# Half of one row tile of w2 sent to partitions 0 to 63 by two 32-partition transfers

## The chip, the cores and the metric

The kernel runs on one core of one Trainium2 chip. The metric is the device time of one execution in microseconds (us); the time before is 774.0 us, the median of three runs (773.93 to 774.09). All data is float32.

## What is computed

One decoding step (batch 2, one token each, model width D = 1024). The input x is normalised, and three terms are added: x itself, an attention term over a cache of 32768 positions (4 key/value heads, 32 query heads of width 128), and a feed-forward term with hidden width F = 3584:

```python
xn = _layernorm(x)
h  = silu(xn @ w1)              # w1 is 1024 x 3584
out = x + attention(xn, k_cache, v_cache, wq) @ wo + h @ w2   # wo 4096 x 1024, w2 3584 x 1024
```

The caches and the weights are 331 MB, each read once; every token's arithmetic is small beside that.

## The kernel before, in words

Everything large passes through three buffers of 128 partitions x 64 KB (bufA, bufB, bufC), filled by transfers that SyncE issues in program order (function `load`, line 205; each transfer has a semaphore of its own count). First wq and w1 are streamed and multiplied: `first(u)` makes a [32 x 512] product per column block, `second(u)` turns it with identity matmuls so that the hidden values stand on partitions; line 194 copies them to `pre`, and lines 213 to 219 make hT = silu of them, one column group of 32 per row tile of 128 hidden values (28 tiles). Then eight loop turns stream the keys and values. After the loop the 32 row tiles of wo and the 28 row tiles of w2 (each 128 rows x 1024 columns, 4 KB per partition) are multiplied by oT and hT.

The work around the change is this tail. SyncE issues the pieces in the order of lines 344 to 346 and 376; the queue is one, so pieces move in that order. bufA is filled last: w2's tiles 16 to 27 in pieces of 1024 KB (four, two tiles each), 512 KB (tiles 24, 25 and 26, one each), and the last tile, 27, in four pieces of 128 KB. Each piece has a semaphore, and TensorE waits for it just before the tile that needs it (line 359). Tiles up to number 55 of the 60 (wo's 32 count first) add into a [128 x 512] sum `acc2`, in two halves of 512 columns; VectorE adds the residual to it once (line 368, result in `ob`). Tiles 56 to 59 add into `acc`, [128 x 256]: four groups of 32 output partitions, group j holding columns 256 j to 256 j + 255 of the result. Just before tile 58 the matmuls of lines 356 to 358 fold `ob` into `acc` and so wait for VectorE. Tile 57, w2's third last (row tile 25), is multiplied at lines 370 and 371: four matmuls of 256 columns, all 128 partitions. The last tile is multiplied in four steps of 64 columns per group, one for each 128 KB piece (lines 382 to 386). Then ScalarE copies `acc` to `ot` (line 388) and stores it (line 389).

One float32 matmul of the code stands as two MATMUL records in the trace, each with a weight load (PEld).

Of the kernel before, what the change touches and what calls it, by code (L numbers as in the profile page):

```python
# [8 lines left out]
B, HQ, HKV, SK, DH, D, F = 2, 32, 4, 32768, 128, 1024, 3584  # L9
P = 128  # L10
REP = HQ // HKV
W = 16384
# [2 lines left out]
SUB = 4096  # L15
N1 = F // 512
FT = F // P
QW = D // 4
LOOPS = HKV * B
EPS = 1e-5  # L20
# [31 lines left out]
        self.eng.sem_inc(token, -n)  # L52


def gqa_plus_mlp_kernel(nc, x, kt, v, wq, wo, w1, w2, out):


    pe, dve, act, pool = (Stream(nc, e, n) for e, n in
                          ((nc.tensor, "pe"), (nc.vector, "dve"), (nc.scalar, "act"), (nc.gpsimd, "pool")))
# [3 lines left out]
    def sem(name):  # L63
        sems.append(nc.alloc_semaphore(name))
        return sems[-1]

    def sb(name, *shape):
        return nc.alloc_sbuf_tensor(name, shape, F32).ap()

    def bank(name):  # L70
        return nc.alloc_psum_tensor(name, (P, 512), F32).ap()

    bufA, bufB, bufC = (sb(n, P, W) for n in ("bufA", "bufB", "bufC"))
    ldA, ldB, ldC, ldx, ldr, done = (sem(n) for n in ("ldA", "ldB", "ldC", "ldx", "ldr", "done"))
    tq, tps, trm, tgd, te, tls, tob = (sem(n) for n in ("tq", "tps", "trm", "tgd", "te", "tls", "tob"))
    ident, ones, sel, fold = sb("ident", P, P), sb("ones", P, P), sb("sel", P, 32), sb("fold", P, 64)
# [4 lines left out]
    stats, mv, ln = sb("stats", B, 2, nc.vector.BN_STATS_DIM), sb("mv", B, 2), sb("ln", B, 6)  # L81
    qall = sb("qall", P, LOOPS, REP)
    qT = sb("qT", P, 160)
    oT, hT = sb("oT", P, HQ, 32), sb("hT", P, FT, 32)
    pre, sig, rsig = (sb(n, P, FT, B) for n in ("pre", "sig", "rsig"))
    pr = [sb(f"pr{i}", P, 512) for i in range(2)]
    ob, ot = sb("ob", P, 512), sb("ot", P, QW)
    mx, ls = sb("mx", P, NC, REP), sb("ls", P, NC, REP)
# [4 lines left out]
    ps = [pair[a // 2][:, a % 2 * 512:(a % 2 + 1) * 512] for a in range(2 * NC)]  # L93
    po, acc, smA, smB = (bank(n) for n in ("po", "acc", "smA", "smB"))
    acc = acc[:, :QW]

    def mm(o, lhsT, rhs, start=True, stop=True):
        return nc.tensor.matmul(o, lhsT, rhs, start=start, stop=stop)  # L98
# [20 lines left out]
    V = nc.vector  # L119
# [5 lines left out]
    for i in range(2):  # L125
        t = dve.mark(V.bn_stats(stats[:, i, :], xt[:, i * 512:(i + 1) * 512]))
    dve.wait(t)
    t = dve.mark(V.bn_aggr(mv, stats))
    var, std, y0, t0, t1, rstd = (ln[:, i:i + 1] for i in range(6))
    dve.wait(t)  # L130
    t = dve.mark(V.tensor_scalar_add(var, mv[:, 1:2], EPS))
    act.wait(t)
    t = act.mark(nc.scalar.activation(std, var, AF.Sqrt))
    for f in (lambda: V.reciprocal(y0, std), lambda: V.tensor_mul(t0, y0, y0), lambda: V.tensor_mul(t1, t0, var),
# [4 lines left out]
        t = dve.mark(f())  # L139
# [5 lines left out]
    for k in range(KT):  # L145
        m = mm(px[:, k, :], xn[:, k * P:(k + 1) * P], ident[:B, :B])
    t = pe.mark(m)
# [27 lines left out]
    def second(u):  # L175

        parts = blocks[u][2]
        n = 32 * parts
        o = ps[2 + u % 2][:, :8 * parts].rearrange("p (i j b) -> p i j b", i=4, b=B)
        pe.wait(copied[u])  # L180
        if u >= 2:
            pe.wait(read[u - 2])
        for i in range(4):
            m = mm(o[:, i], pr[u % 2][:n, i * P:(i + 1) * P],
                   ident[:n, :n].rearrange("p (j m) -> p j m", m=32)[:, :, :B])
        dve.wait(pe.mark(m))
        if u < 2:
            for j in range(2):
                h = 2 * u + j
                m = V.tensor_copy(qall[:, B * h:B * (h + 1), :].rearrange("p b (j i) -> p b j i", j=2),  # L190
                                  o[:, :, 2 * j:2 * j + 2, :].rearrange("p i j b -> p b j i"))
        else:
            at = 16 * (u - 2)
            m = V.tensor_copy(pre[:, at:at + 4 * parts, :].rearrange("p (j i) b -> p j i b", i=4),
                              o.rearrange("p i j b -> p j i b"))
        read.append(dve.mark(m))

    for u in range(4):
        first(u)
        if u:  # L200
            second(u - 1)
    second(3)


    def load(buf, src, s, *ticks):
        for of, n in ticks:
            sp.wait_ge(of.sem, n)
        sp.dma_start(buf, src).then_inc(s, 16)  # L208
# [5 lines left out]
    t = act.mark(nc.scalar.activation(sig, pre, AF.Exp, scale=-1.0))  # L214
    for f in (lambda: V.tensor_scalar_add(sig, sig, 1.0), lambda: V.reciprocal(rsig, sig),
              lambda: V.tensor_mul(hT[:, :, ::16], pre, rsig)):
        dve.wait(t, zs)
        t = dve.mark(f())
# [28 lines left out]
    for it in range(LOOPS):  # L247
        h, b = divmod(it, B)
        for c in range(NC):
            dve.wait(tick(it, c))  # L250
            t = dve.mark(V.transpose(st[:, 2 * c:2 * c + 2].rearrange("p a j m -> p (a j m)"), pair[c]))  # L251
            dve.wait(t)
            m = V.tensor_reduce(mx[:, c, :], st[:, 2 * c:2 * c + 2].rearrange("p a j (r m) -> p m (a j r)", r=4),  # L253
                                AX.X, ALU.max)
            if c == 0:
                m.then_inc(tps, 1)
        m = dve.mark(m)
# [5 lines left out]
        t = dve.mark(V.tensor_reduce(gm, smA[:REP, :P], AX.X, ALU.max))  # L263
# [3 lines left out]
        t = dve.mark(V.tensor_copy(gmax[:, 0, :], smB[:, :REP]))  # L267
# [6 lines left out]
        for c in range(NC):  # L274
            dve.wait(tick(it, 4 + c))
            m = V.tensor_reduce(ls[:, c, :], e8[c].rearrange("p n m -> p m n"), AX.X, ALU.add)  # L276
# [6 lines left out]
        t = dve.mark(V.reciprocal(rl, smA[:, :REP]))  # L283
# [8 lines left out]
    with nc.tensor.While(lambda: nc.tensor.snap(turn) < LOOPS):  # L292
        pe.take(tq)
        for a in range(4):
# [4 lines left out]
            for r in range(4):  # L299
                for q4 in range(4):  # L300
                    n = (4 * (a % 2) + q4) * 4 + r
                    m = mm(ps[a][32 * q4:32 * q4 + 32, :], qT[:, 32 * r:32 * r + 32], buf[:, n * 512:(n + 1) * 512],
                           r == 0, r == 3)
# [6 lines left out]
        for a in range(4):  # L310
# [4 lines left out]
            for j in range(16):  # L315
                q4, n = j % 4, 16 * (a % 2) + j
                m = mm(po[32 * q4:32 * q4 + 32, :], st[:, a, j, :], buf[:, n * 512:(n + 1) * 512],
                       a == 0 and j < 4, a == 3 and j >= 12)
# [5 lines left out]
        for r in range(4):  # L324
            m = mm(smB[:, :REP], ob[:, r * P:(r + 1) * P], sel[:, REP * r:REP * (r + 1)], r == 0, r == 3)
# [8 lines left out]
    def stream(buf, src, cuts, *ticks):  # L334

        for lo, hi in zip(cuts, cuts[1:]):
            s = sem(f"piece{len(pieces)}")
            load(buf[:, lo:hi], src[:, lo:hi], s, *ticks)
            pieces.append((hi, s))
            yield hi, s  # L340

    lo = 11 * D
# [8 lines left out]
    def tiles(buf, ends, at, n):  # L351
        for i in range(n):
            t = at + i
            if t == PAIRED + 2:
                pe.wait(i_fold, i_sums)
                for j in range(4):
                    mm(acc[32 * j:32 * j + 32, :], fold[:, 32 * (j // 2):32 * (j // 2) + 32],
                       ob[:, (j % 2) * QW:(j % 2 + 1) * QW], False, False)
            pe.wait((next(s for hi, s in ends if hi >= (i + 1) * D), 16))
            lhsT, w = oT[:, t, :] if t < HQ else hT[:, t - HQ, :], buf[:, i * D:(i + 1) * D]  # L360
            if t < PAIRED:
                for half in range(2):
                    g = 2 * (t % 2) + half
                    m = mm(acc2[32 * g:32 * g + 32, :], lhsT, w[:, half * 512:(half + 1) * 512],
                           t < 2, t >= PAIRED - 2)
                if t == PAIRED - 1:
                    dve.wait(pe.mark(m), (ldr, 32))
                    i_sums = dve.mark(V.tensor_add(ob, acc2, xres))
            else:
                for j in range(4):  # L370
                    m = mm(acc[32 * j:32 * j + 32, :], lhsT, w[:, j * QW:(j + 1) * QW], t == PAIRED, False)
        return m

    pe.wait(i_oT, i_hT)
    i_wo0 = pe.mark(tiles(*plan[0], 16))
    ends = [*stream(bufA, w2[:, W:], (0, 2 * D, 4 * D, 6 * D, 8 * D, 9 * D, 10 * D, lo, lo + QW, lo + 2 * QW,
                                      lo + 3 * QW, lo + D), i_wo0)]
    for buf, loaded, at in plan[1:]:
        tiles(buf, loaded, at, 16)
    tiles(bufA, ends, 48, 11)  # L380
    f = QW // 4
    for u in range(4):
        pe.wait((ends[7 + u][1], 16))
        for j in range(4):
            m = mm(acc[32 * j:32 * j + 32, u * f:(u + 1) * f], hT[:, FT - 1, :],
                   bufA[:, lo + (4 * u + j) * f:lo + (4 * u + j + 1) * f], False, u == 3)
# [36 lines left out]
```

## Time and profile before

| | |
|---|---|
| median of 3 runs | 774.0 us |
| the profiled execution | 773.97 us |
| its span, first to last instruction | 772.5 us |
| outside the span | 1.47 us |
| HBM read | 331.37 MB, 429 GB/s over the span |
| TensorE busy | 52% |
| queue of SyncE, share of 16 DMA engines | 99.4% |

The page gives busy time by engine, the busy share of the 16 DMA engines in 40 slices, and the chain of work that ended last. Views with a window give the same for a stretch: the DMA share there is the mean over the 16 DMA engines of the time in which they move packets (it can stand a little over 1 in a short window, since a packet is counted whole in one place), and GB/s is what they moved. A timeline merges like instructions, gives the start of the first, how long the group took, and in brackets how long the engine stood idle before and what released it.

### The profile page before, as it was taken

To read this page: it belongs to the slowest core of one execution; us is meant where nothing else is said; L and a number is where in the kernel's file an instruction comes from. 1 tells how busy PE (TensorE), PEld (TensorE's weight loads), DVE (VectorE), ACT (ScalarE), POOL (GpSimd) and SP (SyncE) were. 2 spreads that over 40 slices of the span, in tenths; PEclk is the share of its full clock that TensorE was granted. 3 is DMA by queue.
4 is the path that set the end of the run, shared out by engine and by line. 5 is a ranking of instruction groups with operands and counts; after the bars stand their busy time and mean duration, and the time that the engine had idled before them with its cause. 6 is when DMAs were issued, how large, how long until landed. Compare 5 with 4: busy or idle time off the path is not lost. (4 is left out here: it accounts for less than half of the span.)

```text
span 772.5 us, 5904 instructions
## 1 busy us (share of the span) xinstructions
PE 404.3 (52%) x2736; PEld 127.9 (17%) x2736; DVE 120.7 (16%) x153; ACT 27.3 (4%) x33; POOL 3.0 (0%) x10
## 2 busy tenths in 40 slices
PE   1455545465446455545465446455545465446476
PEld 1111211121112111111121112111111121112111
DVE  2000013111311131113111311131113111311000
ACT  0000100000100010000000100000000000100000
POOL 1000000000000000000000000000000000000000
PEclk9966766766766766766766766766766766766768
DMA  9999999999999999999999999999999999999997
GB/s 388 434 432 432 434 435 434 435 434 434 434 434 434 435 434 431 434 434 434 431 431 434 434 434 434 434 434 434 434 434 431 434 434 434 434 434 434 418 418 320
DMA packets 7379, 331.48 MB, mean 429 GB/s; under 512 B 830, under 2 KB 1350, under 8 KB 1740
## 3 DMA queue, kind: packets, MB, share of 16 engines
q1 hardware_dynamic: 7344, 331.35, 99.4%
q8 instruction: 6, 0.10, 0.0%
q10 hardware_dynamic: 28, 0.02, 0.0%
q14 instruction: 1, 0.01, 0.0%
HBM read 331.37 MB, written 0.01 MB: 429 GB/s over the span
## 5 line engine op out<-in xcount | busy, mean ns | idle before, releaser
L98 PE MATMUL po<-bufB,st 128*32 128x512 f32 x512 | 75.5, 755 | 80.5 <-PEq L52 80.5
L98 PE MATMUL ps<-bufB,qT 128*32 128x512 f32 x512 | 75.0, 751 | 79.3 <-PEq L52 79.3
L98 PE MATMUL ps<-bufA,qT 128*32 128x512 f32 x512 | 75.6, 756 | 48.4 <-PEq L52 48.4
L98 PE MATMUL po<-bufA,st 128*32 128x512 f32 x512 | 74.4, 746 | 36.6 <-PEq L52 36.6
L276 DVE TENSOR_REDUCE ls<-st 128x8 f32<-128x1024 f32 x16 | 31.7, 1984 | 230.8 <-PE po L98 230.8
L251 DVE STREAM_TRANSPOSE st<-ps 128x1024 f32<-128x1024 f32 x16 | 20.0, 1250 | 248.0 <-PE ps L98 248.0
L98 PEld LDWEIGHTS po<-bufB,st 128*32 128x32 f32 x512 | 20.6, 135 | 135.3 <-issue 135.3
L98 PEld LDWEIGHTS ps<-bufB,qT 128*32 128x32 f32 x512 | 20.4, 134 | 133.8 <-issue 133.8
L98 PEld LDWEIGHTS ps<-bufA,qT 128*32 128x32 f32 x512 | 20.7, 135 | 96.7 <-issue 96.7
L98 PEld LDWEIGHTS po<-bufA,st 128*32 128x32 f32 x512 | 20.5, 134 | 83.9 <-issue 83.9
L253 DVE TENSOR_REDUCE mx<-st 128x8 f32<-128x1024 f32 x16 | 31.7, 1980 | 0.6
L273 ACT ACTIVATE st<-st 128x1024 f32<-128x1024 f32 x16 | 16.9, 1056 | 359.1 <-DVE st L272 358.5
L98 PE MATMUL ps<-bufB,xnT 128*32 128x512 f32 x112 | 18.5, 745 | 14.6 <-PEq L52 14.6
L98 PE MATMUL smA<-ident,rm 128*8 128x128 f32 x16 | 4.1, 348 | 29.4 <-PEq L52 29.4
L272 DVE TENSOR_TENSOR st<-st,gmax 128x1024 f32<-128x1024 f32 x16 | 18.9, 1221 | 0.3
L98 PE MATMUL ps<-bufC,oT 128*32 128x512 f32 x64 | 9.4, 753 | 10.5 <-DMA bufC<-in_wo 10.5
L98 PE MATMUL ps<-bufC,xnT 128*32 128x512 f32 x64 | 9.5, 758 | 10.1 <-DMA bufC<-in_w 10.1
L98 PE MATMUL smA<-lsum,ones 128*128 128x8 f32 x16 | 3.5, 291 | 19.2 <-PEq L52 19.2
L281 ACT COPY ob<-po 128x512 f32<-128x512 f32 x8 | 4.7, 585 | 237.9 <-PE po L98 237.9
L98 PE MATMUL smB<-sel,ob 128*128 128x8 f32 x64 | 13.0, 333 | 0.0
L98 PEld LDWEIGHTS smB<-sel,ob 128*128 128x128 f32 x64 | 12.6, 293 | 0.0
L98 PE MATMUL ps<-bufB,hT 128*32 128x512 f32 x64 | 9.6, 763 | 3.9 <-DMA bufB<-in_w 3.9
(65 smaller groups left out, 100.5 us busy)
## 6 DMA issues: line engine op xcount, KB each, us to landing
bufB<-in_w SPq DMA_DIRECT2D x1, 6144.0 KB, 25.5
bufB<-in_w SPq DMA_DIRECT2D x1, 5632.0 KB, 41.8
bufA<-in_w SPq DMA_DIRECT2D x4, 1024.0 KB, 35.4
bufB<-in_w SPq DMA_DIRECT2D x1, 2560.0 KB, 47.7
bufA<-in_w SPq DMA_DIRECT2D x3, 512.0 KB, 40.0
bufA<-in_w SPq DMA_DIRECT2D x4, 128.0 KB, 23.5
bufA<-in_kt SPq DMA_DIRECT2D x8, 29.2
bufB<-in_kt SPq DMA_DIRECT2D x8, 29.0
```

What stands on the lines that cost most here:

```text
L98: return nc.tensor.matmul(o, lhsT, rhs, start=start, stop=stop)
L251: t = dve.mark(V.transpose(st[:, 2 * c:2 * c + 2].rearrange("p a j m -> p (a j m)"), pair[c]))
L253: m = V.tensor_reduce(mx[:, c, :], st[:, 2 * c:2 * c + 2].rearrange("p a j (r m) -> p m (a j r)", r=4), AX.X, ALU.max)
L272: act.wait(dve.mark(V.tensor_sub(e8[c], e8[c], gmax.to_broadcast([P, 128, REP]))))
L273: nc.scalar.activation(e8[c], e8[c], AF.Exp, scale=SCALE).then_inc(te, 1)
L276: m = V.tensor_reduce(ls[:, c, :], e8[c].rearrange("p n m -> p m n"), AX.X, ALU.add)
L281: nc.scalar.copy(ob, po).then_inc(tob, 1)
```

## The change

The columns 512 to 1023 of w2's row tile 25 (256 KB: 128 rows of 2 KB) are no longer loaded as 128 partitions x 2 KB. They come from a new input w2x, in which row p and row p + 64 stand side by side: 64 rows of 4 KB, to bufA's columns 12 D to 13 D, partitions 0 to 63. Two transfers of 32 partitions each fetch them, and the source of each is written as eight groups of four rows that do not lie next to each other in memory (`"r e n -> e r n"`). The first half of the tile is loaded as before with rows of 2 KB in place of 4 KB. The tile's second half is then multiplied with 64 partitions at a time: two matmuls for each of the two column groups, in place of one. The hidden values of rows 64 to 127 of that tile are needed on partitions 0 to 63 too: `second(3)` gets one more matmul, and `pre`, `sig`, `rsig` and `hT` one more tile.

```diff
+LOW = FT - 3
-    oT, hT = sb("oT", P, HQ, 32), sb("hT", P, FT, 32)
-    pre, sig, rsig = (sb(n, P, FT, B) for n in ("pre", "sig", "rsig"))
+    oT, hT = sb("oT", P, HQ, 32), sb("hT", P, FT + 1, 32)
+    pre, sig, rsig = (sb(n, P, FT + 1, B) for n in ("pre", "sig", "rsig"))
...
+        if u == 3:
+            j, i = divmod(LOW - 16, 4)
+            xo = ps[2 + u % 2][:, 8 * parts:8 * parts + B]
+            m = mm(xo, pr[u % 2][:n, i * P + 64:i * P + 192], ident[:n, 32 * j:32 * j + B])
...
+            if u == 3:
+                m = V.tensor_copy(pre[:, FT, :], xo)
...
+            if t == HQ + LOW:
+                pe.wait(*((s, 16) for s in low))
...
                 for j in range(4):
+                    if t == HQ + LOW and j >= 2:
+                        for n in range(2):
+                            at2 = lowA + n * 512 + (j - 2) * QW
+                            m = mm(acc[32 * j:32 * j + 32, :], hT[:64, FT if n else LOW, :], bufA[:64, at2:at2 + QW],
+                                   False, False)
+                        continue
...
-    ends = [*stream(bufA, w2[:, W:], (0, 2 * D, 4 * D, 6 * D, 8 * D, 9 * D, 10 * D, lo, lo + QW, lo + 2 * QW,
-                                      lo + 3 * QW, lo + D), i_wo0)]
+    lowA, low = 12 * D, [sem("low0"), sem("low1")]
+    ends = [*stream(bufA, w2[:, W:], (0, 2 * D, 4 * D, 6 * D, 8 * D, 9 * D, 9 * D + D // 2), i_wo0)]
+    for n in range(2):
+        load(bufA[32 * n:32 * n + 32, lowA:lowA + D], w2x[n].rearrange("r e n -> e r n"), low[n])
+    ends += [(10 * D, ends.pop()[1])]
+    ends += [*stream(bufA, w2[:, W:], (10 * D, lo, lo + QW, lo + 2 * QW, lo + 3 * QW, lo + D))]
...
+    arrays["w2x"] = lay(arrays["w2"][:, LOW * D + D // 2:(LOW + 1) * D], (2, 2, 8, 4, D // 2), (1, 3, 2, 0, 4),
+                        (2, 4, 8, D))
```

## Rows read from the trace of the kernel before

**Rows 1.** The page: span, DMA in 40 slices, packets, queues.
```profile
span 772.5 us, 5904 instructions
...
DMA  9999999999999999999999999999999999999997
GB/s 388 434 432 432 434 435 434 435 434 434 434 434 434 435 434 431 434 434 434 431 431 434 434 434 434 434 434 434 434 434 431 434 434 434 434 434 434 418 418 320
...
q1 hardware_dynamic: 7344, 331.35, 99.4%
q8 instruction: 6, 0.10, 0.0%
```
**Rows 2.** Chain of waits from 766 us on: start us, us, what.
```profile
727.58 40.84 DMA bufA<-in_w
768.42 0.04 issue
768.46 0.99 PE acc L98 x24
...
769.48 0.68 PE acc L98 x16
```
**Rows 3.** Busy time by stretch, the last DMA work: columns in the first line.
```profile
core 0: us, PE busy (x) PEld busy (x) DVE busy (x) ACT busy (x) POOL busy (x), PEclk, DMA share, GB/s
...
767.00:767.50 0.50, 0.50 (x12) 0.22 (x12) 0.32 (x1) 0.00 (x0) 0.00 (x0) 0.69 1.03 356
767.50:767.75 0.25, 0.25 (x12) 0.15 (x8) 0.00 (x0) 0.00 (x0) 0.00 (x0) 1.00 0.80 283
767.75:768.00 0.25, 0.25 (x12) 0.06 (x4) 0.00 (x0) 0.00 (x0) 0.00 (x0) 1.00 0.53 180
768.00:768.25 0.25, 0.25 (x8) 0.00 (x0) 0.00 (x0) 0.00 (x0) 0.00 (x0) 1.00 0.50 172
768.25:768.50 0.25, 0.07 (x8) 0.04 (x6) 0.00 (x0) 0.00 (x0) 0.00 (x0) 1.00 0.46 160
768.50:768.75 0.25, 0.25 (x8) 0.12 (x8) 0.00 (x0) 0.00 (x0) 0.00 (x0) 1.00 0.40 139
768.75:769.00 0.25, 0.25 (x16) 0.18 (x8) 0.00 (x0) 0.00 (x0) 0.00 (x0) 1.00 0.36 123
769.00:769.25 0.25, 0.25 (x20) 0.17 (x12) 0.00 (x0) 0.00 (x0) 0.00 (x0) 1.00 0.27 94
769.25:769.50 0.25, 0.23 (x12) 0.07 (x10) 0.00 (x0) 0.00 (x0) 0.00 (x0) 1.00 0.02 4
```
**Rows 4.** The same view, while the 1024 KB and the 512 KB pieces move.
```profile
757.00:758.00 1.00, 1.00 (x16) 0.26 (x12) 0.00 (x0) 0.00 (x0) 0.00 (x0) 1.00 1.04 434
...
765.00:766.00 1.00, 1.00 (x8) 0.10 (x4) 0.00 (x0) 0.00 (x0) 0.00 (x0) 0.50 1.01 405
```
**Rows 5.** Timeline of weight loads from 764 us on.
```profile
764.62 0.20 PEld L98 LDWEIGHTS ps<-bufA,hT 128*32 128x32 f32 x8 [2.33 <-DMA bufA<-in_w]
765.90 0.15 PEld L98 LDWEIGHTS acc<-bufA,hT 128*32 128x32 f32 x4 [1.08 <-DMA bufA<-in_w]
...
767.18 0.19 PEld L98 LDWEIGHTS acc<-bufA,hT 128*32 128x32 f32 x8 [0.65 <-DMA bufA<-in_w]
767.47 0.34 PEld L98 LDWEIGHTS acc<-ob,fold 128*32 128x32 f32 x8
768.46 0.16 PEld L98 LDWEIGHTS acc<-bufA,hT 128*32 128x32 f32 x8 [0.66 <-DMA bufA<-in_w]
768.82 0.47 PEld L98 LDWEIGHTS acc<-bufA,hT 128*32 128x32 f32 x16 [0.20 <-DMA bufA<-in_w]
769.47 0.16 PEld L98 LDWEIGHTS acc<-bufA,hT 128*32 128x32 f32 x8 [0.18 <-DMA bufA<-in_w]
769.79 0.16 PEld L98 LDWEIGHTS acc<-bufA,hT 128*32 128x32 f32 x8 [0.16 <-DMA bufA<-in_w]
```
**Rows 6.** Timeline of TensorE's matmuls from 764 us on.
```profile
764.62 1.93 PE L98 MATMUL ps<-bufA,hT 128*32 128x512 f32 x8 [1.43 <-DMA bufA<-in_w]
766.33 1.53 PE L98 MATMUL acc<-bufA,hT 128*32 128x256 f32 x16
767.68 0.60 PE L98 MATMUL acc<-ob,fold 128*32 128x256 f32 x8
768.46 1.65 PE L98 MATMUL acc<-bufA,hT 128*32 128x256 f32 x40 [0.17 <-DMA bufA<-in_w]
```
**Rows 7.** Groups by shape from 745 us on: busy, mean ns of one | idle before.
```profile
L98 PE MATMUL acc<-ob,fold 128*32 128x256 f32 x8 | 0.6, 379 | 0.0
```
**Rows 8.** Timelines of VectorE and of ScalarE in the tail.
```profile
766.62 0.69 DVE L368 TENSOR_TENSOR ob<-ps,xres 128x512 f32<-128x512 f32 x1 [55.22 <-PE ps L98]
...
770.18 0.37 ACT L388 COPY ot<-acc 128x256 f32<-128x256 f32 x1 [62.88 <-PE acc L98]
770.58 0.64 ACTq L389 DMA_DIRECT2D out_y<-ot  x1
```
**Rows 9.** SyncE's issues of bufA's last pieces: timeline; page, us to landing.
```profile
724.84 33.22 SPq L208 DMA_DIRECT2D bufA<-in_w  x11
...
bufA<-in_w SPq DMA_DIRECT2D x4, 128.0 KB, 23.5
```
**Rows 10.** Timelines of TensorE and VectorE around `second(3)`.
```profile
86.24 1.95 PE L98 MATMUL ps<-ident,pr 128*128 128x8 f32 x16
96.85 9.46 PE L98 MATMUL ps<-bufA,qT 128*32 128x512 f32 x64 [8.66 <-PEq L52]
...
88.23 0.18 DVE L194 COPY pre<-ps 128x24 f32<-128x24 f32 x1 [0.70 <-PE ps L98]
```

More of the change, by code (lines that the diff above doesn't have):

```diff
@@ L52, in take, with gqa_plus_mlp_kernel @@
         self.eng.sem_inc(token, -n)
-def gqa_plus_mlp_kernel(nc, x, kt, v, wq, wo, w1, w2, out):
+def gqa_plus_mlp_kernel(nc, x, kt, v, wq, wo, w1, w2, w2x, out):
     pe, dve, act, pool = (Stream(nc, e, n) for e, n in
```

## Prediction, made before the changed kernel was run

> **What bounds the kernel now.** I read the page first: SyncE's queue fills 99.4% of what 16 DMA engines can do, every slice of the DMA line but the last stands at 9, and the rate is 434 GB/s nearly throughout [rows 1]. The change adds no bytes and takes none away, so it can't touch those 770 us; it can only touch how the stream ends. The chain of waits says the same: from 727.58 to 768.42 us it is one stretch of bufA's pieces, then TensorE's last matmuls [rows 2]. So next I cut the last microseconds into quarters. The reader is to see the DMA share there: 1.03 up to 767.5, 0.80, 0.53, then 0.50 at 768.00 to 768.25, and from there a slow fall to 0.02 after 769.25 [rows 3]. A share of 0.50 of 16 engines is eight engines at work and eight that have nothing left. SyncE's queue gave all sixteen the same bytes, so eight run behind the other eight by about 1.3 us, and the last pieces wait for those eight. The share summed from 767.75 on is 0.25 x (0.53 + 0.50 + 0.46 + 0.40 + 0.36 + 0.27 + 0.02) = 0.64 us. Spread evenly over sixteen engines the same work would end at 768.39 in place of about 769.26. So 0.87 us (0.11%) is the most that any redistribution of these bytes can bring, and the stake of the whole change.
>
> After the last packet TensorE follows closely: its last wait for a piece ends at 769.79 [rows 5], ScalarE's copy starts at 770.18 and the store is issued at 770.58 [rows 8]. That end, 0.39 us and what follows, stays as it is.
>
> **The change part by part.** The *transfers*. By the diff a half tile of 256 KB is taken from all 128 partitions and given to partitions 0 to 63 in rows of 4 KB, eight groups to a transfer. I read the eight groups as eight engines, each with four rows of each transfer; the trace of before has no such transfer, so bounds follow. Rates of one engine: rows of 8 KB, 434 GB/s at share 1.04, so 434 / (16 x 1.04) = 26.1 GB/s; rows of 4 KB, 405 / (16 x 1.01) = 25.1 [rows 4]; rows of 1 KB, 139 / (16 x 0.40) = 21.7 [rows 3]. For rows of 2 KB I take 24.4, between the last two and nearer the 4 KB row. Before, each engine moves 32 KB of the tile: 1.31 us. After, eight move 16 KB in rows of 2 KB, 0.67 us, and the other eight that and 32 KB in rows of 4 KB: 0.67 + 1.31 = 1.98 us. So eight engines gain 0.64 us and eight lose 0.67. If the eight that gain are those that are late, both groups end near 768.6 to 768.7 and the last landing is 0.6 us earlier. If any of those that lose is late, the end is 0.67 us later. From both sides: 0.87 us earlier (the sum above) to, with all of it on one engine, 256 KB / 25.1 = 10.4 us later; I take 0.6 us earlier, and say at the rivals why.
>
> Which partitions an engine serves no row here shows. The Trainium skill, "DMA: Bandwidth & Descriptors", sections "Why a DMA increments its semaphore by 16 and not by 1" and "The descriptor swizzle", gives the number of engines as the largest up to 16 that divides the slowest dimension of both sides, here 8, takes the lowest numbered ones, and has those write partitions 0 to 63. By it the reading above holds, and the engines that are relieved are numbers 8 to 15.
>
> *SyncE's queue*: two issues more, 13 in place of 11. The 11 take 33.22 us from 724.84, the last issue ending at 758.06, since the queue pushes back; the last pieces are issued a median 23.5 us ahead of their landing [rows 9]. Ten descriptors more on half of the engines, each of some 0.16 us (4 KB at 25.1), delay the last issue by 1 or 2 us, with over 9 us of cover. Nothing. Gone would be that cover only if the issue of the new form took some 9 us.
>
> *TensorE in the tail*. Tile 57 gets two matmuls more; column groups run side by side, so what counts is the longest group: four passes in place of two. A pass of 256 columns at a granted clock of 1.00 (2.4 GHz): the fold's 8 records take 0.60 us, one alone 0.379 [rows 6, 7], so its second pass starts 0.22 later. Two more passes: 0.44 us. Does that show? Tile 57 could start earlier, but TensorE works without a gap from 766.33 to 768.28 (766.33 + 1.53, then the fold, 767.68 + 0.60 [rows 6]), because up to 767 it runs at 0.50, 1.2 GHz [rows 3, 4]. So the fold moves from 767.68 to 768.12, past VectorE's sum, which is done at 766.62 + 0.69 = 767.31 [rows 8]. Tile 58 follows two passes later, at 768.56 (768.46 before, where it stood 0.17 us waiting for data [rows 6]); its data would be there at 767.9. It takes 0.44, so the first step of the last tile starts at 769.00, and each step has 8 weight loads in 0.16 us [rows 5]: the fourth starts at 769.48. Before, it started at 769.79, by its landing. So on TensorE's side the gain is 0.31 us; on the landings' side 0.6 us. The steps may be closer than 0.16 once all data is there, so I take the middle, 0.45 us. The two added waits stand at tile 57, and what is queued behind them is the fold and tile 58, counted already.
>
> *The front end*. One matmul and one copy more in `second(3)`. Its matmuls end at 88.19; the next ones start at 96.85 after 8.66 us of idle time [rows 10]. A copy is 0.18 us. Nothing, in 8.66 us of cover.
>
> **Sum.** 773.97 (the profiled execution; the median of the runs is 774.0) - 0.45 = 773.5 us.
>
> **Rivals.** (1) *The late engines are on the side that gets more.* For it: nothing in the trace names the engines, and the six 16 KB instruction blocks [rows 1] are each one more load on some engine; what falls behind so has no reason to lie on one side of partition 64. One late engine among the loaded eight is enough, so this rival needs only a mixed set. Against it: the plateau is at 0.50 and the fall begins only after it [rows 3], two groups of eight, the number that a half of the partitions gives. Price: the last landing 0.67 us later, TensorE follows with its slack to spare: 773.97 + 0.67 = 774.6 us. This is the one on the other side; it decides as soon as one loaded engine ends after 769.26 - 0.67 = 768.59 in the trace of before. The Trainium skill speaks for this side: "SBUF — State Buffer", section "Door 1: The DMA port swizzle", says that 64 partitions reach only half the ports and so half the rate, and advises one transfer over all 128. By it alone 256 KB through half the engines costs 0.65 us more. The trace agrees on the rate (172 GB/s at share 0.50 [rows 3]); it does not show that the other half would stand idle meanwhile.
>
> (2) *The change doesn't do what it says*: the two transfers are spread over all sixteen engines. Then each moves 0.67 + 0.65 us as before, the landings stay, and TensorE's 0.44 us of passes uses the 0.17 us of waiting before tile 58 and the gaps behind it: 774.0 us, 0.0 to +0.1. Against it speaks the odd form of the source.
>
> (3) *TensorE becomes the bound through its clock.* It is at 0.50 up to 767 and rises in 767.0 to 767.5 [rows 3], after working without a gap since 764.62 [rows 5, 6]. If it stayed at 1.2 GHz, the ten passes from 767.18 on (four, the fold's two, tile 58's two, the last tile's eight short ones counted as two) would take 4.4 us: an end of matmuls at 771.6 against 770.18, so 775.4 us. Against it: up to 767.18 TensorE's work is the same as before.
>
> (4) *The new form falls on one engine*: up to 10.4 us on the tile's landing, about 784 us. Nothing in the trace speaks for it.
>
> **How the numbers follow.** Forecast 0.55, (1) 0.30, (2) 0.08, (3) 0.03, (4) 0.02, gains beyond the bound 0.02. The likeliest gives 773.5, by itself 773.1 (the bound of 0.87) to 773.8 (TensorE's side at its worst). Rival (1) must be in the range, so it runs from 773.1 to 774.8. A difference under 0.2%, 1.55 us, counts here as no change, for that is about what a measurement of this kernel can tell; forecast and rivals (1) to (3) all lie within it. Slower: (4) and the upper end of (3), 0.04. Faster: 0.02, only beyond the bound. Within: 0.94.
>
> **What would show it.** Right: in the quarters after 767.5 the DMA share stays near 1 until about 768.3 and then falls steeply, without the plateau at 0.50; the last wait of TensorE for a piece ends near 769.2, or the last steps stand without waits. Wrong by (1): the plateau at 0.50 is there longer and the last DMA work ends near 769.9. By (2): the tail's shares as before. By (3): a granted clock of 0.50 after 767.5. At the front, the first kt matmuls still at 96.85. A time under 773.1 or over 774.8 would say that something outside the tail moved.

## The result: 774.9 us, slower by 0.8 us (0.1%), and the profile after

The changed kernel takes 774.9 us (median of 22 runs, 774.49 to 777.35); the kernel before, beside it, 774.09 us (22 runs, 773.92 to 774.82). The ratio is 1.0014, with a 95% interval of 1.0008 to 1.0021; it lies above the 1.0010 of the medians, as the ratio of the means does (775.28 to 774.13), since four runs took 776.49 to 777.35. I had forecast 773.5 in a range up to 774.8: the sign was wrong and the range ended 0.1 us short. The class "within 0.2%" was right, but rivals (1) to (3) lie in it as well as the forecast, so it speaks for none of them. The profiled execution took 775.01 us, its span is 773.6 us against 772.5 [rows 1].

The page of the changed kernel shows the same stream: the same 331.35 MB on SyncE's queue.

```profile
span 773.6 us, 5920 instructions
...
q1 hardware_dynamic: 7424, 331.35, 99.2%
q8 instruction: 7, 0.11, 0.1%
```

(The seventh instruction packet starts at 771.2 us, behind the stream.)

The busy time by stretch of the tail, the view of [rows 3] (after PEclk stand the DMA share and GB/s):

```profile
core 0: us, PE busy (x) PEld busy (x) DVE busy (x) ACT busy (x) POOL busy (x), PEclk, DMA share, GB/s
...
767.75:768.00 0.25, 0.25 (x3) 0.02 (x1) 0.00 (x0) 0.00 (x0) 0.00 (x0) 0.50 0.81 287
768.00:768.25 0.25, 0.25 (x4) 0.00 (x0) 0.00 (x0) 0.00 (x0) 0.00 (x0) 0.50 0.79 275
768.25:768.50 0.25, 0.25 (x2) 0.00 (x0) 0.00 (x0) 0.00 (x0) 0.00 (x0) 0.50 0.64 221
768.50:768.75 0.25, 0.25 (x4) 0.17 (x4) 0.00 (x0) 0.00 (x0) 0.00 (x0) 0.53 0.43 148
768.75:769.00 0.25, 0.25 (x4) 0.14 (x4) 0.00 (x0) 0.00 (x0) 0.00 (x0) 1.00 0.14 49
769.00:769.25 0.25, 0.25 (x6) 0.11 (x2) 0.00 (x0) 0.00 (x0) 0.00 (x0) 1.00 0.14 49
769.25:769.50 0.25, 0.25 (x6) 0.00 (x0) 0.00 (x0) 0.00 (x0) 0.00 (x0) 1.00 0.07 25
769.50:769.75 0.25, 0.25 (x6) 0.13 (x8) 0.00 (x0) 0.00 (x0) 0.00 (x0) 1.00 0.01 4
```

The plateau at 0.50 is gone, as forecast: the share stands near 0.8 to 768.25, and by 768.75 most of the work is done, 0.5 us earlier than before. But a new plateau stands behind it: 0.14 of sixteen is two engines, and they move packets until about 769.6, 0.3 us later than the last ones of before (769.33 in the trace; the forecast reckoned with 769.26).

The trace says which two. It keeps the time of each increment of a transfer's semaphore, and each engine that moves a part of the transfer makes one when that part has landed: 16 for a piece over 128 partitions, 8 for each small transfer, as the eight groups were meant. For the piece just ahead of the small transfers nine increments come from 764.56 to 765.24 us, then seven at 765.83, at 766.17 and from 766.44 to 766.57. The eight of the first small transfer follow six of the nine, and the two at 765.83 and 766.17, each 0.63 to 0.65 us later. So two of the eight engines that got more were late already, the five latest were relieved, and the last landing comes at 770.05 in place of 769.75.

The end, though, no longer hangs on the landings. The timeline:

```profile
766.37 3.32 PE L100 MATMUL acc<-bufA,hT 128*32 128x256 f32 x20
...
767.55 0.22 PEld L100 LDWEIGHTS acc<-bufA,hT 128*32 128x32 f32 x4 [0.98 <-DMA bufA<-in_w]
768.58 0.63 PEld L100 LDWEIGHTS acc<-bufA,hT 64*32 64x32 f32 x8 [0.81 <-issue]
769.62 0.16 PEld L100 LDWEIGHTS acc<-ob,fold 128*32 128x32 f32 x8 [0.41 <-issue]
769.62 0.64 PE L100 MATMUL acc<-ob,fold 128*32 128x256 f32 x8
...
770.08 1.06 PE L100 MATMUL acc<-bufA,hT 128*32 128x256 f32 x40
771.21 0.37 ACT L411 COPY ot<-acc 128x256 f32<-128x256 f32 x1 [64.87 <-PE acc L100]
```

and the chain of waits (start us, us, what):

```profile
726.90 37.72 DMA bufA<-in_w
764.62 0.04 issue
764.67 1.94 PE ps L100 x8
766.60 0.85 PE acc L100 x8
767.46 0.13 issue
767.59 3.60 PE acc L100 x60
```

Before, the chain went through the pieces up to 768.42 [rows 2]; now it leaves them at 764.62, and everything after is TensorE. The row to look at is the weight load at 768.58: 64 rows, 0.81 us after the one before, with nothing to wait for but TensorE itself. Tile 57 begins at 767.59 and the fold at 769.62, 2.03 us later, where before it was 0.5 us (767.18 to 767.68 [rows 5, 6]). It also begins later, since its small transfers have landed only at 767.45; its piece of before had at 767.14. The waits of 0.66, 0.20, 0.18 and 0.16 us for the last pieces [rows 5] are gone: all data is there before TensorE asks. The granted clock is 0.50 (1.2 GHz) up to 768.5 here; before, it rose after 767 [rows 3]. It also fell earlier. By stretch, the changed kernel and then the kernel before:

```profile
762.00:764.00 2.00, 1.84 (x8) 0.20 (x8) 0.00 (x0) 0.00 (x0) 0.00 (x0) 0.50 0.97 395
```
```profile
762.00:764.00 2.00, 1.07 (x8) 0.16 (x8) 0.00 (x0) 0.00 (x0) 0.00 (x0) 0.97 0.97 395
```

TensorE had been busy for 1.36 us of 757 to 759 here, for 2.00 before, and in neither from 761 to 762. Why the clock fell earlier no run shows.

### The profile page after: what moved, and what is told of

Read it like the earlier page. It is cut to its first block, busy times and chain, and to the rows that moved or that the text cites. A ratio compares the mean times of both kernels' runs of the same rounds, so it can differ in the third digit from the quotient of the medians.

```text
span 773.6 us, 5920 instructions
## 1 busy us (share of the span) xinstructions
PE 394.7 (51%) x2742; PEld 124.7 (16%) x2742; DVE 120.8 (16%) x154; ACT 27.3 (4%) x33; POOL 3.0 (0%) x10
## 3 DMA queue, kind: packets, MB, share of 16 engines
q1 hardware_dynamic: 7424, 331.35, 99.2%
## 5 line engine op out<-in xcount | busy, mean ns | idle before, releaser
L100 PE MATMUL po<-bufB,st 128*32 128x512 f32 x512 | 72.4, 729 | 80.1 <-PEq L53 80.1
L100 PE MATMUL ps<-bufA,qT 128*32 128x512 f32 x512 | 72.5, 730 | 51.3 <-PEq L53 51.3
L100 PE MATMUL ps<-bufA,oT 128*32 128x512 f32 x64 | 9.5, 758 | 6.7 <-DMA bufA<-in_wo 6.7
L100 PE MATMUL ps<-bufA,xnT 128*32 128x512 f32 x64 | 9.7, 775 | 5.0 <-PEq L53 5.0
(66 smaller groups left out, 106.7 us busy)
```

## The experiments

Two theories. **T**: TensorE has become the bound, by the form of the 64-row matmuls and by its clock. **L**: the landings are later, since some of the engines that get more bytes were late already. All times beside runs of the kernel before on the same chip (774.0 to 774.1 us).

**e1_transfers_only** and **e2_matmuls_only** split the change.

```diff
 e1
-                    if t == HQ + LOW and j >= 2:
+                    if False:
 e2 (the pieces of before, no wait for low)
-    lowA, low = 12 * D, [sem("low0"), sem("low1")]
+    lowA = 9 * D
```

> The changed kernel with its transfers, but tile 57 multiplied as before: four matmuls of 128 rows, so its columns 512 to 1023 get old data of bufA. Theory T (TensorE is the bound at the end: the 64-row matmuls run behind the 128-row ones, not beside them, and at a granted clock of 0.50): the last matmul ends within 0.4 us of the last landing again, and the time is 774.1 to 774.5 us, what is left over 774.1 being a later landing. Rival L (landings: engines that were late already get more bytes): the matmuls' form changes nothing, 774.9 us as the changed kernel.

> The transfers of before (tile 57 as one piece of 512 KB), with the changed kernel's matmuls: the second half of tile 57 is multiplied by twice two 64-row matmuls that read partitions 0 to 63 of that piece, so rows 64 to 127 of these columns are left out and the lower ones are used twice. Theory T: tile 57 takes 1.3 us at a granted clock of 1.00 to 2.0 us at 0.50 in place of 0.5, the end of TensorE moves by 0.2 to 0.8 us: 774.3 to 774.9 us. Rival L: 774.1 us, as before.

Measured: e1 774.37 us, ratio 1.0005 (0.9996 to 1.0014); e2 774.29 us, 1.0008 (0.9999 to 1.0017). Each alone is about a third to a half of the loss and at the edge of what can be measured: both intervals hold 1. In e1 TensorE waits for its last piece again; timeline of weight loads, then the DMA share:

```profile
764.91 0.20 PEld L100 LDWEIGHTS ps<-bufA,hT 128*32 128x32 f32 x8 [2.29 <-DMA bufA<-in_w]
...
768.87 1.07 PEld L100 LDWEIGHTS acc<-bufA,hT 128*32 128x32 f32 x32 [0.20 <-DMA bufA<-in_w]
770.10 0.16 PEld L100 LDWEIGHTS acc<-bufA,hT 128*32 128x32 f32 x8 [0.16 <-DMA bufA<-in_w]
```
```profile
769.25:769.50 0.25, 0.25 (x12) 0.14 (x4) 0.00 (x0) 0.00 (x0) 0.00 (x0) 1.00 0.14 49
```

The last wait ends at 770.10 against 769.79 [rows 5], 0.31 us later, with two engines left at the end as in the changed kernel. But the weight load at 764.91, for the last piece of 1024 KB, ahead of the change, is 0.29 us later than before too (764.62 [rows 5]), so this execution shows next to no shift in the tail; e3 and e11 below, at 764.58 and 764.59, do. In e2 nothing of the transfers is changed, and TensorE is late; timeline of its matmuls:

```profile
766.38 3.27 PE L100 MATMUL acc<-bufA,hT 128*32 128x256 f32 x20
769.57 0.64 PE L100 MATMUL acc<-ob,fold 128*32 128x256 f32 x8
```

The fold starts at 769.57 in place of 767.68 [rows 6], as in the changed kernel. This profiled execution took 775.05, though: six of e2's eleven runs took 774.13 to 774.29 and five 774.66 to 776.78, so the trace stands for the longer ones; its granted clock is 0.50 up to 769. Both theories hold, each for a part.

**e3_all_rows** keeps the transfers and makes the four matmuls with 128 rows.

```diff
-                            m = mm(acc[32 * j:32 * j + 32, :], hT[:64, FT if n else LOW, :], bufA[:64, at2:at2 + QW],
+                            m = mm(acc[32 * j:32 * j + 32, :], hT[:, FT if n else FT + 1, :], bufA[:, at2:at2 + QW],
...
```

> The changed kernel, but the four matmuls of 64 rows are made with 128 rows, the lower 64 meeting zeros in hT (two more small VectorE instructions at the front). The transfers are the same. Theory T: passes run beside each other again, four per column group in place of six one behind the other, and TensorE ends 0.5 to 0.9 us earlier: 774.2 to 774.6 us. Rival L: 774.9 us.

Measured: 774.6 us, 1.0010 (1.0001 to 1.0020), the upper end of what T expected. Timelines:

```profile
767.58 0.65 PE L100 MATMUL acc<-bufA,hT 128*32 128x256 f32 x8 [1.07 <-DMA bufA<-in_w2x]
768.01 0.41 PE L100 MATMUL acc<-ob,fold 128*32 128x256 f32 x2
768.05 0.39 PE L100 MATMUL acc<-bufA,hT 128*32 128x256 f32 x2
```
```profile
764.58 0.16 PEld L100 LDWEIGHTS ps<-bufA,hT 128*32 128x32 f32 x8 [2.33 <-DMA bufA<-in_w]
...
770.08 0.16 PEld L100 LDWEIGHTS acc<-bufA,hT 128*32 128x32 f32 x8 [0.16 <-DMA bufA<-in_w]
```

With 128 rows the column groups work beside each other, and the fold of the first two groups starts at 768.01 while the other two still multiply. (The granted clock is 1.00 in this tail.) The last piece is waited for again, at 770.08, 5.50 us behind the load at 764.58 where before it was 5.17 (769.79 and 764.62 [rows 5]): TensorE's part is away, L's part is left, 0.33 us here.

**e4_sixteen_engines** lets the two small transfers run on sixteen engines.

```diff
-        load(bufA[32 * n:32 * n + 32, lowA:lowA + D], w2x[n].rearrange("r e n -> e r n"), low[n])
+        load(bufA[32 * n:32 * n + 32, lowA:lowA + D], w2x[n], low[n])
...
```

> The changed kernel, with the rows of each small transfer lying next to each other in memory in place of eight groups of four separate rows; by my reading each transfer then runs on sixteen engines, two rows each. The matmuls are the same. Theory T: TensorE stays the bound, 774.5 to 775.0 us, with the plateau of DMA share at 0.50 back in the tail. Rival L: the landings are those of before, 774.0 to 774.2 us.

Measured: 778.57 us, 1.0058 (1.0045 to 1.0072): both expectations missed by 3.5 us or more. The profiled execution took 777.36, the shortest of the five. By stretch:

```profile
763.00:764.00 1.00, 0.28 (x4) 0.00 (x0) 0.00 (x0) 0.00 (x0) 0.00 (x0) 1.00 0.95 381
...
765.00:766.00 1.00, 1.00 (x8) 0.00 (x0) 0.00 (x0) 0.00 (x0) 0.00 (x0) 0.50 1.01 176
766.00:767.00 1.00, 0.83 (x8) 0.17 (x8) 0.27 (x1) 0.00 (x0) 0.00 (x0) 0.50 1.08 323
767.00:768.00 1.00, 0.91 (x8) 0.03 (x4) 0.42 (x1) 0.00 (x0) 0.00 (x0) 0.51 0.95 190
768.00:769.00 1.00, 0.00 (x0) 0.00 (x0) 0.00 (x0) 0.00 (x0) 0.00 (x0) 1.00 1.07 187
```

The share stays at 1 and the rate falls to 176 to 190 GB/s, with 323 in one stretch between: sixteen engines are busy and move as much as eight do (172 GB/s at share 0.50 [rows 3]). By the increments, sixteen for each small transfer here, the nine early engines move their part of the two up to 766.7, the seven late ones up to 769.3, and an engine takes about 0.7 us for 8 KB, as long as for 16 KB in the changed kernel (0.64). So partitions 0 to 63 take only about half of the rate, from sixteen engines as from eight, and engines that wait there also hold up the pieces behind: the last landing is 2.0 us later than before (771.75). That is not the whole of the 4.5 us. Tile 57 waits for its small transfers until 769.47, and from there TensorE takes 4.05 us to its end without a wait for a piece, in place of 3.60. The eight separate groups are what keeps the rate from falling so: my reading of them was right. The Trainium skill, "SBUF — State Buffer", section "Door 1: The DMA port swizzle", says that 64 partitions reach half of the ports; the trace agrees, with 176 to 190 GB/s beside 381 to 434.

**e5_early_half** makes the change to row tile 20, **e6_busy** adds eleven unread matmuls in the waits of TensorE; **e7_quarter_transfers** and **e8_whole_transfers** vary the size, with e1's matmuls.

```diff
 e5
-LOW = FT - 3
+LOW = FT - 8
...
 e6
+                if 48 <= t < PAIRED - 2 and t % 2:
+                    for k in range(3):
+                        mm(ps[2], ident, w[:, :512])
...
+                    for k in range(2):
+                        mm(ps[2], ident, w[:, :512])
 e7
-        load(bufA[32 * n:32 * n + 32, lowA:lowA + D], ...
+        load(bufA[32 * n:32 * n + 32, lowA:lowA + D // 2], ...
 e8
+        load(bufA[32 * n:32 * n + 32, lowA:lowA + 2 * D], ...
```

> The same change made to row tile 20 (tile 52 of 60) in place of 25: same bytes moved, the same two extra matmuls of 64 rows, but where TensorE waits over 1 us for each piece. Theory T + L (two costs: the landings 0.3 us later because engines already late get more bytes, and TensorE's longer tile 57 in the tail): the TensorE part is hidden, the landings stay, 774.3 to 774.5 us, no run above 775.5. Rival (the extra matmuls alone): 774.0 to 774.1 us. Rival (transfers alone): 774.9 us.

> The changed kernel with eleven matmuls more whose result nobody reads (128 columns by 512, into an unused bank), in the gaps where TensorE waits for the pieces of tiles 48 to 56. Theory T with the clock: the granted clock is 1.00 in the tail in most runs, TensorE's part of the loss shrinks to what the landings leave, 774.4 to 774.6 us, and the runs of 776 to 777 us go. Rival (the clock has no part in it): 774.9 us or more, the runs of 776 to 777 stay.

> Transfers only, as in e1 (128-row matmuls, the last columns of tile 57 get old data), but a quarter of the tile, 128 KB, is given to partitions 0 to 63. Theory L (late engines on the loaded side, no fixed cost): each engine's shift is 0.33 us, late loaded engines end 0.33 us later, late relieved ones 0.33 us earlier, 773.7 to 774.1 us. Rival F (a fixed cost of two more small transfers, or of writing to half of the partitions): 774.3 to 774.4 us, as e1.

> Transfers only, as in e1, but the whole tile, 512 KB, is given to partitions 0 to 63 (tile 57 gets old data). Theory L: each loaded engine moves 1.31 us more than before, the late ones end 0.9 to 1.0 us later than the last landing of before, 774.9 to 775.1 us. Rival F: 774.3 to 774.5 us, as e1.

e5: 774.69 us, 1.0011 (1.0002 to 1.0020). Above its expectation, with two runs, 775.59 and 777.33, that should not have been there. Its profile waits for the last piece at 770.50, 0.71 us later than [rows 5], so there the landings make the whole of it. That is more than in e3, with the same bytes: which engines are late, and by how much, differs from one execution to the next.

e6: 778.96 us, 1.0065 (1.0051 to 1.0079), a miss of my making: the unread matmuls cost more than the gaps hold. Timeline:

```profile
769.49 1.98 PE L100 MATMUL ps<-bufA,ident 128*128 128x512 f32 x4
771.40 2.05 PE L100 MATMUL acc<-bufA,hT 128*32 128x256 f32 x20
773.38 0.64 PE L100 MATMUL acc<-ob,fold 128*32 128x256 f32 x8
```

Four records take 1.98 us, so TensorE ran 4 us behind its data. It still gives one number: tiles 56 and 57 take 1.98 us to the fold's start with all data there.

e7: 774.35 us, 1.0003 (0.9994 to 1.0012), above L's range and in that of rival F. But its profile, an execution of 774.93, ran the tail at a granted clock of 0.50 and ended on TensorE, not on a landing, so e7's time doesn't tell L from F. The increments do: an engine takes 0.33 us for its part of a small transfer in e7, 0.64 in the changed kernel, 1.25 in e8, in step with the bytes, and no fixed cost is left over. e8: 775.22 us, 1.0016 (1.0006 to 1.0025), a little above L's range and far above F's. Its profile, of 776.17, is its longest run, and TensorE at 0.50 ends it; the tail of its transfers:

```profile
769.25:769.50 0.25, 0.25 (x8) 0.22 (x4) 0.00 (x0) 0.00 (x0) 0.00 (x0) 0.50 0.23 78
769.50:769.75 0.25, 0.25 (x10) 0.05 (x4) 0.00 (x0) 0.00 (x0) 0.00 (x0) 0.50 0.21 74
...
770.25:770.50 0.25, 0.25 (x8) 0.11 (x4) 0.00 (x0) 0.00 (x0) 0.00 (x0) 0.50 0.04 12
```

Twice the bytes, and the last engines (here about three, 0.21 to 0.23) work to about 770.4 in place of 769.6.

**e9_light_busy**, **e10_before_busy** and **e11_all_rows_busy** repeat e6 with four unread matmuls in place of eleven: on the changed kernel, on the kernel before, and on e3.

```diff
+                if 48 <= t < PAIRED - 2 and t % 2:
+                    mm(ps[2], ident, w[:, :512])
...
                     i_sums = dve.mark(V.tensor_add(ob, acc2, xres))
+                    mm(ps[2], ident, w[:, :512])
```

> The changed kernel with four matmuls more whose result nobody reads (128 columns by 512, one after each of the tiles 49, 51, 53 and 55), so that TensorE is not behind its pieces but busier. Theory T with the clock: granted clock 1.00 in the tail, tile 57 takes 1.55 us as in e6 in place of 2.0, TensorE ends within 0.2 us of what the landings allow: 774.3 to 774.5 us and no run over 775.5. Rival (the clock has no part): 774.9 us, single runs of 776 to 777 as the changed kernel.

> The kernel before with the same four matmuls: control. Every theory: 773.9 to 774.2 us, since there the last landing ends the chain and not TensorE; if the clock also costs the kernel before something in its slower runs, its highest runs (774.4 to 774.8) go.

> The changed transfers with both costs of TensorE taken away: 128-row matmuls as in e3 and the four extra matmuls of e9. Theory T + L: what is left is the landing of the late engines among those that get more, 774.2 to 774.4 us, with a narrow spread. Rival (the transfers cost nothing): 773.5 to 774.1 us.

e9: 774.7 us, 1.0009 (1.0000 to 1.0018), above the 774.5 expected, highest run 775.34; the four runs from 776.49 to 777.35 of the changed kernel have no like here, which with eleven runs can be chance. e10: 774.17 us, 1.0002 (0.9993 to 1.0012), as expected, though its highest run (774.58) is no lower than before's (774.22). e11: 774.57 us, 1.0008 (0.9999 to 1.0017), 774.26 to 774.82, above the 774.4 expected. The extra matmuls may cost some of that themselves; beside e10, which has them too, e11 is 0.40 us longer, and e9 another 0.13. In e9 the granted clock is 1.00 (2.4 GHz) throughout the tail, and tile 57 is long all the same; timelines of matmuls and of weight loads, from its longest run:

```profile
768.15 1.62 PE L100 MATMUL acc<-bufA,hT 128*32 128x256 f32 x12 [0.43 <-DMA bufA<-in_w2x]
769.69 0.64 PE L100 MATMUL acc<-ob,fold 128*32 128x256 f32 x8
```
```profile
768.12 0.17 PEld L100 LDWEIGHTS acc<-bufA,hT 128*32 128x32 f32 x4 [0.88 <-issue]
768.70 0.58 PEld L100 LDWEIGHTS acc<-bufA,hT 64*32 64x32 f32 x8 [0.41 <-issue]
769.69 0.16 PEld L100 LDWEIGHTS acc<-ob,fold 128*32 128x32 f32 x8 [0.41 <-issue]
```

That is 1.54 us from 768.15 to the fold at 769.69, of which the clock has no share. The 64-row weight loads begin 0.41 us after the 128-row ones have ended, and the fold's as long after those. Tile 57 also starts late: the small transfers hold it up to 768.15, where its piece of before came at 767.18 [rows 5]. (0.41 us of that were there before the tail: in this run the load for the last 1024 KB piece comes at 765.03, where it was 764.62 [rows 5].) e11 has neither cost of TensorE. Its weight loads:

```profile
764.59 0.16 PEld L100 LDWEIGHTS ps<-bufA,hT 128*32 128x32 f32 x8 [1.20 <-DMA bufA<-in_w]
...
770.22 0.16 PEld L100 LDWEIGHTS acc<-bufA,hT 128*32 128x32 f32 x8 [0.16 <-DMA bufA<-in_w]
```

TensorE waits for the last landing, 0.43 us later than before (770.22 and 769.79). That is L by itself.

**e12_one_block_more** asked why engines are late at all.

```diff
+    for k in range(64):
+        mm(po[:, :8], ident, ident[:, :8])
```

> e1 (the changed transfers, 128-row matmuls) with 64 small matmuls more on TensorE at the front, between the weights and the loop, where it idles for over 7 us: 256 instructions, one 16 KB block of its program. It asks why engines are late. Theory B (each instruction block is fetched by another engine, in turn, and leaves that engine behind): the page shows 7 instruction packets by the time the stream ends in place of 6, the last one falls on one more engine of the loaded eight, the DMA share in the last half microsecond of the stream is 0.19 to 0.20 (three engines) in place of 0.14 (two), and the time is 774.3 to 774.7 us. Rival (lateness has another origin): share 0.14 there, 774.3 to 774.4 us, as e1.

Measured: 785.22 us, 1.0150 (1.0136 to 1.0163). The time answers nothing: the 64 matmuls met a granted clock of 0.50 to 0.56 and took far longer than the gap, so bufA came free late and the queue ran dry. Two views, timeline and by stretch:

```profile
87.82 24.90 PE L100 MATMUL po<-ident 128*128 128x8 f32 x128
```
```profile
115.00:120.00 5.00, 5.00 (x36) 1.27 (x32) 0.00 (x0) 0.00 (x0) 0.00 (x0) 0.71 0.02 3
...
779.25:779.50 0.25, 0.25 (x8) 0.13 (x8) 0.00 (x0) 0.00 (x0) 0.00 (x0) 1.00 0.21 74
```

The tail's last share is 0.21, three engines, as theory B expected. But e8 shows as much without the extra block, so the share settles nothing. The increments do, and for B. In the trace of the kernel before all sixteen engines end the piece at 41 us within 0.7 us of each other. Six instruction packets of 16 KB move during the stream [rows 1], starting at 46.2, 73.0, 106.7, 142.8, 721.1 and 752.6 us, and in the first piece that ends well behind each of them one more engine is late, by some 1.4 us, and stays late. A seventh engine falls behind between 249 and 269 us with no packet beside it. Twelve of the other thirteen traces show the same, six steps with the six packets and one without. The thirteenth is e12: behind its dry stretch all sixteen end within 0.6 us again (at 144 us), then one more is late after each of the three packets that follow, and one without a packet: four in all, three of them among the loaded eight.

## Why the prediction was wrong, point by point

*What bounds the kernel* held: the loss lies in the last 5 us, and the bytes before it are untouched. The front end held too (the next matmuls start at 96.92, before at 96.85), and so did SyncE's queue (its last issue ends at 759.82, before at 758.06).

*The transfers* is the step that failed: "I take 0.6 us earlier", on the condition that the eight engines that gain are those that are late. The shifts of 0.64 and 0.67 us were about right, since most of the work did end 0.5 us earlier and the plateau of eight engines went. But the late engines were not one half: of the eight that got more, two were late already, and a landing waits for the last engine. In the changed kernel and in e11 the last landing is 0.30 and 0.43 us later, in place of 0.6 earlier. I read the plateau at 0.50 as two halves of the partitions; the row says only how many engines are late, not which. Rival (1) said just that and had 0.30, with instruction blocks as its ground, which e12 bears out; its price, 0.67, was the worst case. The price follows from the lag: in the changed kernel the later of the two loaded late engines was 0.40 us ahead of the latest of all (766.17 and 766.57), so its 0.67 leave 0.27. All ten traces with eight loaded engines have two or three late ones among them, and in each this sum gives the measured shift of the last landing against the last 1024 KB piece ahead of the change, to 0.12 us: 0.02 in e1, 0.09 in e7, 0.26 in the changed kernel, 0.46 in e11, 0.62 in e5, 1.09 in e8. The sign I had named for (1), a longer plateau at 0.50, did not show; a mixed set leaves a low one.

*TensorE in the tail* was mis-sized. I counted four passes side by side, 0.44 us more. Measured, tile 57 takes 1.54 us at a granted clock of 1.00 (e9) and 2.03 us in the changed kernel, mostly at 0.50, in place of 0.5. The 64-row matmuls start only when the 128-row ones are through, then run four passes, and the fold waits for them in turn: six passes in a row, 1.32 us by the 0.22 of the forecast, and two changes. With 128 rows throughout (e3) that goes. At 1.2 GHz it is longer still, rival (3), which I gave 0.03 on the ground that TensorE's work is the same up to 767.18; but the clock fell earlier in this run, at the pair of tiles before. And the sum had no term for the small transfers themselves: they, too, land as late as the loaded late engines bring them, and tile 57 waits for them (0.31 us later than its piece of before in the changed kernel).

So the loss of 0.8 us has two parts: later landings (774.37 with e1, 774.57 with e11, against 774.0) and TensorE (774.29 with e2, against 774.0). With both, TensorE ends last, and the 0.3 us between the changed kernel and e3 or e11 is its part on top, 0.13 of it with the clock at 1.00 (e9 and e11). The mechanisms are read from the traces; the sizes are small beside the scatter of the runs, and how much of TensorE's part is the clock's is argued, not shown. Nor is the cause of the runs of 776 to 777 us: they came with the changed kernel, e2, e3, e5 and once with e8, and not with e9 or e11, but no profile caught one above 776.17.

No variant beat the kernel before. By number the late engines are not known, so which half of the partitions would be the better one to relieve stays open; and so does the one step without an instruction packet.

## What to carry to other kernels

A DMA share below 1 at the end counts the engines that are late; it does not name them, and moving bytes off a group pays only if no late engine is in the group that gets them. The increments of a semaphore, one from each engine, tell how late each is, and a transfer on half of the engines shows whose they are. Before a split tile is put where the last wait is short, count its matmuls as if they ran one behind the other, unless a row shows that form side by side. A tail in which TensorE has 0.2 us of slack at one clock has none at the other (e7).

## What the runs showed of the hardware

Sixteen engines writing to partitions 0 to 63 move 176 to 190 GB/s, and what is queued behind is held up with them: the last landing 2.0 us later for 256 KB (e4). In a queue that never runs dry one DMA engine falls some 1.4 us behind at each 16 KB instruction packet and stays behind to the end (thirteen traces); a dry stretch wipes that out (e12). Matmuls of 64 rows and of 128 rows in different column groups did not run beside each other, 128-row ones did (e9, e3). An unread float32 matmul of 128 x 128 by 512 costs about 1 us at 2.4 GHz (1.98 us for the two of e6), and two records of 8 columns each still cost 0.39 us together at 0.50 to 0.56 (24.90 us for 64 matmuls, e12).
